# Block-sorted attention with a squared-ReLU layer: the last outputs in parts of 256, 128 and 128 columns, and the sorted values written to DRAM in two halves

## The chip, the cores and the metric

The kernel runs on one core of one Trainium2 chip. The metric is the device time of one execution in microseconds (us). The engines are named as the profile names them: PE (matrix engine), PEld (its weight loads), DVE (vector), ACT (scalar), POOL (GpSimd) and SP (sync). SP computes nothing here: it issues transfers and waits.

## What is computed

Inputs are q, k and v of shape 4 x 8 x 768 x 64 (batch, head, position, width) in float32, a sort_net of 4 x 8 x 8 x 8, and the weights of a layer from 512 to 2048 and back to 512. Each head's 768 positions are 8 blocks of 96.

```python
P = sort_net                                   # 5 rounds of exp, row and column normalization
for _ in range(5):
    P = np.exp(P - np.max(P, axis=-1, keepdims=True))
    P = P / (np.sum(P, axis=-1, keepdims=True) + 1e-09)
    P = P / (np.sum(P, axis=-2, keepdims=True) + 1e-09)
k_sorted = np.einsum('bhij,bhjcd->bhicd', P, k_b)      # blocks mixed by P
v_sorted = np.einsum('bhij,bhjcd->bhicd', P, v_b)
attn = softmax(q_b @ k_sorted^T / sqrt(64))            # within each block of 96
x = (attn @ v_sorted), heads side by side              # 3072 x 512
h = x @ w_in
g = s * np.maximum(h, 0)**2 + b
out = g @ w_out                                        # 3072 x 512
```

## The kernel before

The order of all instructions is written out by hand; every engine and SP's queue run theirs in the order of the program. The 3072 tokens are eight tiles t of 384 tokens (TG = 384): two for each of the four batches b, each of four blocks.

For a batch, k and v are mixed by P on PE (PD[b] holds P spread over 128 partitions). For batches 2 and 3 the sorted values go this way: `v_rows(b, u)`, six times, multiplies the v tile by PD on PE and DVE copies the product back over v (lines 349 and 351). Then `v_back(b)` writes that tile, RAW["v", b], to a DRAM tile vd in one transfer of 128 partitions x 6144 bytes (line 355), and loads it back in four transfers, one for each pair of z and e, into VS[b % 2] with positions on partitions (line 359). In vd the outermost index is e, then z. Each of the four loads moves 1536 rows of 128 bytes. Directly behind v_back on SP's queue stands `q_dma(b)`, two DMA transposes that make q ready for the scores (line 457), and behind these come the stores of the outputs. POOL's loads of the v of the batch after are held by a copy at line 90 until the transposed q is there.

The scores are `s_piece` (line 381: sc from qt and ks), the values `p_piece` (line 423: pv from vs and at), and two more transposes for each batch (line 449) make their result the input of the layer.

The layer is `ffn1(t)` (line 474, then ACT's relu and DVE's square into gt) and `ffn2(t)`. `ffn2` walks over three groups m of 128 tokens; each group is 16 matmuls of 512 columns into one PSUM tile ops (line 498), then `store`: DVE makes s * ops + bias into a tile ot of SBUF (line 519) and SP stores it (line 522). The pieces of the next batch's attention are put between the matmuls by a table of slots, of which batch 2 and 3 have theirs in tiles 2 to 5. The last two tiles, 6 and 7, have none. In the last tile (`last`) the third group, m = 2, is done as two groups of 16 matmuls of 256 columns (line 511), each with its own `store`.

Buffers that matter: ops comes from psb, two buffers; ot from osb, three, taken in turn, one for each call of `store`. vd has one, v's RAW tiles two.

How SP's transfers are watched: in the trace the landing of SP's transfers is told on eight semaphores, numbers 108, 109, 112, 113, 114, 116, 117 and 118, which they take in this order, in turn. A transfer is issued behind a wait for the one eight back, which used the same semaphore. At the program's end, SP waits for all eight, in the same order, and then for the other engines (line 673). Before, SP issues 52 transfers: sort_net, four of v, 25 output stores, two times one store of vd and four loads of vs, six transposes of q and six of x.

Of the kernel before, what the change touches and what calls it, by code (L numbers as in the profile page):

```python
# [9 lines left out]
FP = mybir.dt.float32  # L10
# [12 lines left out]
def kernel(  # L23
# [12 lines left out]
    nc = tc.nc  # L36
# [6 lines left out]
    d_model = H * D  # L43
    d_ff = moe_w_in.shape[1]
    NF = d_ff // 128
    HB = NB // 2
    TG = HB * BLK
# [22 lines left out]
    psb = ctx.enter_context(tc.tile_pool(name="psb", bufs=2, space=bass.MemoryType.PSUM))  # L70
# [9 lines left out]
    for c in range(0, C2, CV):  # L80
        nc.sync.dma_start(out=v0f[:, c:c + CV, :].rearrange("p c d -> p (c d)"),
                          in_=raw[2][0][:, c * D:(c + CV) * D])

    RAW = {}
# [123 lines left out]
    def q_banks(b, half, engs):  # L208
# [3 lines left out]
        for u in range(2):  # L212
# [13 lines left out]
            out=jsel, in_=ident.rearrange("p (h j z) -> p j h z", h=H, j=NB), axis=AX.XY, op=ALU.add),  # L226
        lambda: nc.vector.tensor_reduce(
            out=bm.rearrange("p (e z a) -> p e z a", e=2, z=2),
            in_=idv.rearrange("p a e j z -> p e z a j"), axis=AX.X, op=ALU.add),
# [122 lines left out]

    def v_back(b):
        vd = drp.tile([2, 2, NG, C2, D], BF, tag="vd", name="vd")
        nc.sync.dma_start(out=vd.rearrange("e z g c d -> (e z g) (c d)"),
                          in_=RAW["v", b].rearrange("p c d -> p (c d)"))
        for z in range(2):
            for e in range(2):
                nc.sync.dma_start(
                    out=VS[b % 2][z * GAP:z * GAP + C2, e * NG:(e + 1) * NG, 0:D],  # L360
                    in_=vd[e, z].rearrange("g c d -> c g d"))
# [130 lines left out]
    def ffn2(t, slots):  # L492
        gt = GT.pop(t)
        last = t == 2 * B - 1
        for m in range(TG // 128 - int(last)):
            ops = psb.tile([128, d_model], FP, tag="b", name="ops")
            for f in range(NF):
                nc.tensor.matmul(out=ops, lhsT=gt[:, f, m * 128:(m + 1) * 128],  # L498
                                 rhs=wo[:, f, :], start=(f == 0), stop=(f == NF - 1))
                if f % 4 == 3:  # L500
                    if f == NF - 1:
                        store(t, m, ops)
                    for p in slots.get(m * 4 + f // 4, ()):
                        p()
        if last:
            m = TG // 128 - 1
            for n0 in range(0, d_model, d_model // 2):
                ns = slice(n0, n0 + d_model // 2)
                ops = psb.tile([128, d_model // 2], FP, tag="b", name="ops")
                for f in range(NF):  # L510
                    nc.tensor.matmul(out=ops, lhsT=gt[:, f, m * 128:(m + 1) * 128],  # L511
                                     rhs=wo[:, f, ns], start=(f == 0), stop=(f == NF - 1))
                store(t, m, ops, ns)
# [3 lines left out]
    def store(t, m, ops, ns=slice(0, d_model)):  # L517
        ot = osb.tile([128, d_model], FP, tag="ot", name="ot")
        nc.vector.scalar_tensor_tensor(out=ot[:, ns], in0=ops, scalar=s_bc, in1=BIAS[0][:, ns],  # L519
                                       op0=ALU.mult, op1=ALU.add)  # L520
        r0 = t * TG + m * 128
        nc.sync.dma_start(out=out[r0:r0 + 128, ns], in_=ot[:, ns])
# [69 lines left out]
    def VB(b): return lambda: v_back(b)  # L592
# [36 lines left out]
    load("v", 2, 6, QT[1][:, NB - 1, 0, 0:1])  # L629
    s0, s1 = halves(1)  # L630
    ffn2(0, s0)
    ffn2(1, s1)
    for b in range(1, B):
        n = b + 1
        s0, s1, u0, u1 = {}, {}, {}, {}
        if n < B:
            load("k", n, 6, XT[2 * b + 1][:, HB - 1, NHP - 1, 0:1])
            load_q_rows(n)
            s0, s1 = halves(n)
            u0 = {i: [VRW(n, i)] for i in range(6)}  # L640
            u0[5] += [VB(n), QD(n)]
            if n + 1 < B:
                u0[5] += [LV(n + 1)]
        ffn1(2 * b, u0)
        ffn1(2 * b + 1, u1)
        ffn2(2 * b, s0)
        ffn2(2 * b + 1, s1)
# [30 lines left out]
```

## Time and profile before

| | |
|---|---|
| median of 3 runs | 223.43 us (222.94 to 223.51) |
| the profiled execution | 223.59 us |
| its span, first to last instruction | 221.8 us |
| granted PE clock over the span | 1.000 |
| v_back of batch 2: store of vd issued, last load of vs landed | 90.8, 109.35 us |
| v_back of batch 3: the same | 139.3, 157.12 us |
| output stores of 256 KB from 201.9 us on, issue to landing | 2.0 us |
| output stores of 128 KB, issue to landing | 1.7 us |
| last output store issued, landed, end of span | 218.95, 220.66, 221.8 us |

Times inside the execution are counted from the span's start. "Landing" is the last count on the transfer's semaphore. A line of a view of the profile gives line of the program, engine, operation, output and inputs by the program's names, shapes and the number of instructions. In the timeline the first two columns are start and length of a run of equal instructions, and in brackets stands the engine's idle time ahead of it and what ended it. SPq is SP's queue: its entries are issues of transfers and waits. In the list of waits the columns are the total, how many, and the longest. A matmul's recorded length contains its way through the array, so that those of a run overlap; the pitch, the distance between starts, is what one costs. The page puts PE at 97% of the span and the granted clock at full speed in each of its 40 slices.

### The profile page before, as it was taken

The page shows a single profiled execution, that of the slowest core. Times are in us where ns is not written, and L with a number is a line of the kernel's source. Part 1 is how long each engine was busy: PE and PEld are TensorE (multiplying, and loading weights), DVE is VectorE, ACT ScalarE, POOL GpSimd, SP SyncE. Part 2 cuts the span into 40 slices and gives each one's busy share as a digit, 9 for nine tenths or more (in the row PEclk, how much of TensorE's full clock was granted, in tenths as well). Part 3 has the DMA queues.
Part 4 walks back from the last instruction along what each step waited for, and adds up shares of the span by engine and source line. Part 5 has one row for each costly group of instructions (what it writes and reads, how often), then busy time and mean ns, then how long its engine had stood idle before and what let it go on. Part 6 is the DMA issues. An engine that isn't in the chain of part 4 may idle for free.

```text
span 221.8 us, 5257 instructions
## 1 busy us (share of the span) xinstructions
PE 214.8 (97%) x2212; PEld 129.6 (58%) x2231; DVE 123.3 (56%) x251; ACT 106.1 (48%) x144; POOL 70.6 (32%) x127
## 2 busy tenths in 40 slices
PE   7999999999999999999999999999999999999993
PEld 5977766555655555666446555655446556654453
DVE  6767457549754767546616677548417744442121
ACT  4677687656144344664622535665424355650000
POOL 7659791669914004930032008800000000000000
PEclk9999999999999999999999999999999999999999
DMA  6999999999999632999999546999911440001212
GB/s 154 280 165 126 125 162 207 204 177 117 116 182 165 183 96 46 138 236 127 91 252 171 138 121 91 236 147 92 221 69 50 121 120 0 0 3 47 95 47 95
DMA packets 66935, 28.92 MB, mean 130 GB/s; under 512 B 51808, under 2 KB 62816, under 8 KB 66912
## 3 DMA queue, kind: packets, MB, share of 16 engines
q0 software_dynamic: 31168, 12.85, 49.6%
q1 hardware_dynamic: 35744, 15.74, 34.3%
q8 instruction: 17, 0.28, 0.6%
q14 instruction: 6, 0.05, 0.1%
HBM read 28.85 MB, written 7.86 MB: 165 GB/s over the span
## 4 chain that ended last, share of the span: by engine, by line
PE 95%; DVE 2%; issue 1%; ACT 0%
PE hps L474 38%; PE ops L498 36%; PE z L132 5%; PE pv L423 4%; PE sc L381 3%; PE ops L511 2%; PE tv L330 2%; PE tp L294 1%; PE tpp L304 1%; PE tvr L349 1%; DVE vs L206 1%; PE tr L440 1%; PE scb L399 1%; PE sc L259 0%; PE pv L417 0%
## 5 line engine op out<-in xcount | busy, mean ns | idle before, releaser
L474 PE MATMUL hps<-xt,wi 128*128 128x384 bf16 x512 | 87.9, 326 | 0.0
L498 PE MATMUL ops<-wo,gt 128*128 128x512 bf16 x350 | 82.4, 379 | 1.5 <-issue 0.8
L486 ACT ACTIVATE rt<-hps 128x768 bf16<-128x768 f32 x64 | 51.8, 811 | 39.5 <-PE hps L474 38.8
L474 PEld LDWEIGHTS <-wi 128*128 128x128 bf16 x512 | 49.0, 98 | 32.6 <-issue 0.4
L487 DVE TENSOR_TENSOR gt<-rt 128x768 bf16<-128x768 bf16 x64 | 35.6, 558 | 41.2 <-ACT rt L486 41.0
L498 PEld LDWEIGHTS <-gt 128*128 128x128 bf16 x368 | 34.0, 98 | 37.2
L519 DVE SCALAR_TENSOR_TENSOR ot<-ops,s_bc,bias 128x512 f32<-128x512 f32 (+1 forms) x25 | 18.2, 729 | 37.9 <-PE ops L498 34.4
L389 ACT ACTIVATE at<-sc 112x768 bf16<-112x768 f32 x24 | 18.1, 808 | 31.8 <-PE sc L381 31.8
L429 DVE TENSOR_TENSOR x<-pv,rec 96x512 bf16<-96x512 f32 x32 | 22.0, 687 | 1.1
L116 POOL DMA_DIRECT2D qtok<-in_q_dram x24 | 18.6, 810 | 0.7 <-DMA rawk<-in_k_dram 0.6
L423 PEld LDWEIGHTS <-at 112*128 112x128 bf16 (+1 forms) x256 | 12.9, 101 | 6.7 <-ACT at L389 1.0
L142 POOL DMA_DIRECT2D wi<-in_moe_w_in_dram x24 | 13.0, 583 | 6.0 <-DMA qh<-in_q_dram 3.1
L423 PE MATMUL pv<-vs,at 112*128 112x66 bf16 (+1 forms) x256 | 13.9, 195 | 0.1
L93 POOL DMA_DIRECT2D rawk<-in_k_dram x21 | 11.2, 551 | 4.3 <-DMA rawv<-in_v_dram 2.0
L132 PE MATMUL z<-zeros 128*64 128x96 bf16 (+2 forms) x129 | 10.8, 257 | 1.3 <-DVE zeros L120 1.2
L93 POOL DMA_DIRECT2D rawv<-in_v_dram x18 | 9.7, 555 | 5.5 <-DMA wo<-in_moe_w_out_dram 4.7
L204 ACT CAST ks<-tpp 64x512 bf16<-64x512 f32 x12 | 8.7, 725 | 4.4 <-DVE ks L206 4.1
L132 PEld LDWEIGHTS <-zeros 128*64 128x64 bf16 (+1 forms) x130 | 8.5, 128 | 3.0 <-DVE zeros L120 1.2
L90 POOL COPY rawk<-xt 128x1 bf16<-128x1 bf16 x2 | 0.4, 190 | 31.1 <-DMA xt<-x 31.1
L428 DVE RECIPROCAL rec<-pv 96x8 f32<-96x8 f32 x32 | 6.4, 200 | 6.4 <-PE pv L423 6.4
L206 DVE CAST ks<-tpp 64x512 bf16<-64x512 f32 x12 | 8.7, 728 | 0.2
L351 DVE CAST rawv<-tvr 128x512 bf16<-128x512 f32 x12 | 8.2, 683 | 0.0
(93 smaller groups left out, 141.6 us busy)
## 6 DMA issues: line engine op xcount, KB each, us to landing
out_dram<-ot SPq DMA_DIRECT2D x23, 256.0 KB, 2.5
rawv<-in_v_dram POOLq DMA_DIRECT2D x18, 128.0 KB, 5.1
rawk<-in_k_dram POOLq DMA_DIRECT2D x18, 128.0 KB, 4.5
qtok<-in_q_dram POOLq DMA_DIRECT2D x24, 96.0 KB, 6.7
wo<-in_moe_w_out_dram POOLq DMA_DIRECT2D x4, 512.0 KB, 10.4
v0f<-in_v_dram SPq DMA_DIRECT2D x4, 384.0 KB, 7.1
vd<-rawv SPq DMA_DIRECT2D x2, 768.0 KB, 6.8
vs<-vd SPq DMA_DIRECT2D x8, 192.0 KB, 7.4
```

Of the source, the lines that this page charges most:

```text
L93: nc.gpsimd.dma_start(out=ti[:, c:c + n, :].rearrange("p c d -> p (c d)"), in_=raw["qkv".index(t)][b][:, c * D:(c + n) * D])
L116: nc.gpsimd.dma_start(out=ti[:, n + h], in_=qv[:, n + h])
L132: nc.tensor.matmul(out=z[0:m, 0:w], lhsT=zeros[:, 0:m], rhs=zeros[:, 0:w], start=True, stop=True)
L142: nc.gpsimd.dma_start(out=wi[:, al, f0:f1], in_=wiv[:, al, f0:f1])
L389: nc.scalar.activation(out=at, in_=sc[0:KR, :, 0:TG], func=AF.Exp, scale=scale)
L423: nc.tensor.matmul(out=pv[0:m, e, n * VW:(n + 1) * VW], lhsT=atf[:, c0:c0 + m], rhs=VS[b % 2][:, e * NG + g0 + n, :], start=True, stop=True)
L429: nc.vector.tensor_tensor(out=x[:, :, hp * 128:(hp + 1) * 128].rearrange("p n (e d) -> p e n d", e=2), in0=pvv[:, :, :, 0:D], in1=rec.unsq ...
L474: nc.tensor.matmul(out=H1[t, i][:, f, 0:TG], lhsT=wi[:, hp, fc:fc + 128], rhs=XT[t][:, :, hp, :], start=(hp == 0), stop=(hp == NHP - 1))
L486: nc.scalar.activation(out=rt, in_=h, func=AF.Relu)
L487: nc.vector.tensor_tensor(out=gt[:, 2 * i:2 * i + 2, :], in0=rt, in1=rt, op=ALU.mult)
L498: nc.tensor.matmul(out=ops, lhsT=gt[:, f, m * 128:(m + 1) * 128], rhs=wo[:, f, :], start=(f == 0), stop=(f == NF - 1))
L519: nc.vector.scalar_tensor_tensor(out=ot[:, ns], in0=ops, scalar=s_bc, in1=BIAS[0][:, ns], op0=ALU.mult, op1=ALU.add)
```

## The change

Three edits, in two functions.

In `v_back` the tile of sorted values is written to DRAM in two transfers of 64 partitions, one for each e, and the four loads go with e outermost, so that both loads of the first half come ahead of those of the second.

In `ffn2`, in the last tile, the output of the second group (m = 1) is evicted and stored in two halves of 256 columns; its matmuls stay 16 of 512 columns.

In the last tile's third group the two parts of 256 columns become three of 256, 128 and 128, each with its 16 matmuls, eviction and store.

```diff
     def v_back(b):
         vd = drp.tile([2, 2, NG, C2, D], BF, tag="vd", name="vd")
-        nc.sync.dma_start(out=vd.rearrange("e z g c d -> (e z g) (c d)"),
-                          in_=RAW["v", b].rearrange("p c d -> p (c d)"))
-        for z in range(2):
-            for e in range(2):
+        for e in range(2):
+            nc.sync.dma_start(out=vd[e].rearrange("z g c d -> (z g) (c d)"),
+                              in_=RAW["v", b][e * 64:(e + 1) * 64].rearrange("p c d -> p (c d)"))
+        for e in range(2):
+            for z in range(2):
                 nc.sync.dma_start(
                     out=VS[b % 2][z * GAP:z * GAP + C2, e * NG:(e + 1) * NG, 0:D],
                     in_=vd[e, z].rearrange("g c d -> c g d"))
...
                 if f % 4 == 3:
-                    if f == NF - 1:
+                    if f == NF - 1 and last and m == TG // 128 - 2:
+                        for n0 in range(0, d_model, d_model // 2):
+                            ns = slice(n0, n0 + d_model // 2)
+                            store(t, m, ops[:, ns], ns)
+                    elif f == NF - 1:
                         store(t, m, ops)
                     for p in slots.get(m * 4 + f // 4, ()):
                         p()
         if last:
             m = TG // 128 - 1
-            for n0 in range(0, d_model, d_model // 2):
-                ns = slice(n0, n0 + d_model // 2)
-                ops = psb.tile([128, d_model // 2], FP, tag="b", name="ops")
+            for n0, w in ((0, 256), (256, 128), (384, 128)):
+                ns = slice(n0, n0 + w)
+                ops = psb.tile([128, w], FP, tag="b", name="ops")
                 for f in range(NF):
                     nc.tensor.matmul(out=ops, lhsT=gt[:, f, m * 128:(m + 1) * 128],
                                      rhs=wo[:, f, ns], start=(f == 0), stop=(f == NF - 1))
```

SP then issues 56 transfers.

## The prediction

> **What bounds the kernel.** I read first the chain of work that ended last, by engine and line, and beside it the busy time of each engine.
>
> ```profile
> PE 214.8 (97%) x2212; PEld 129.6 (58%) x2231; DVE 123.3 (56%) x251; ACT 106.1 (48%) x144; POOL 70.6 (32%) x127
> PE 95%; DVE 2%; issue 1%; ACT 0%
> ```
>
> The chain is the matrix engine nearly from end to end. The list of PE's waits from 100 to 180 us, where both executions of v_back fall, has one entry, and it is not a wait for data:
>
> ```profile
> PE ops L498 <- issue: 0.3, 2, 0.2
> ```
>
> So nothing that v_back delivers makes PE wait now, and a faster v_back has nothing to give. What is left is the end of the span, where PE has run out. The timeline of the last stretch (start, length, engine, line, operation), then SP's waits from 215 us on (total, times, longest):
>
> ```profile
> 214.75 3.66 PE L511 MATMUL ops<-wo,gt 128*128 128x256 bf16 x32
> 214.95 0.75 DVE L519 SCALAR_TENSOR_TENSOR ot<-ops,s_bc,bias 128x512 f32<-128x512 f32 x1 [2.70 <-PE ops L498]
> 216.69 0.48 DVE L519 SCALAR_TENSOR_TENSOR ot<-ops,s_bc,bias 128x256 f32<-128x256 f32 x1 [1.00 <-PE ops L511]
> 218.44 0.48 DVE L519 SCALAR_TENSOR_TENSOR ot<-ops,s_bc,bias 128x256 f32<-128x256 f32 x1 [1.26 <-PE ops L511]
> ...
> 218.95 0.33 SPq L522 DMA_DIRECT2D out_dram<-ot  x1
> ...
> SPq L673 <- DMA out_dram<-ot: 1.1, 1, 1.1
> ```
>
> Behind PE's last matmul stands a serial tail: last eviction 218.44 to 218.92, last store issued 218.95, landed at 220.66 by its landing semaphore, span over at 221.8. The third part of it is SP's instructions at line 673, the program's end, from 220.6 to 221.0 us:
>
> ```profile
> L673 SPq EVENT_SEMAPHORE x5: 28/28/28, 220.7 to 220.9; - x5
> L673 SPq DRAIN  x1: 7/7/7, 221.0 to 221.0; - x1
> ```
>
> Before its last drain SP waits once for each of the eight landing semaphores, always in the order 108, 109, 112, 113, 114, 116, 117, 118. SP's 52 transfers take them in that order in turn, and the last is on 113, the fourth. So the wait that the landing ends is followed by four more, for transfers that landed long ago: 220.675 to 220.917, 0.242 us in which nothing is outstanding.
>
> **The change, part by part: the tail.** Times are from the one profiled execution.
>
> (a) PE. Two groups of 16 matmuls of 256 columns become one of 256 and two of 128. The 256-column pitch is (3.66 - 0.27) / 31 = 0.109 us. A matmul of 128 columns with a fresh 128x128 weight load is in the trace at line 304:
>
> ```profile
> 102.58 1.50 PE L304 MATMUL tpp<-pd,rawk 128*128 128x128 bf16 x24
> ```
>
> Its pitch is (1.50 - 0.22) / 23 = 0.056 us, so the added weight loads stay hidden. The second half began at 216.492; its 32nd narrow matmul starts at 216.492 + 31 x 0.0557 = 218.219, where the last wide one started at 218.130: +0.089. From that start to the eviction it was 0.311, of which the matmul's recorded length falls from 0.272 to 0.219: -0.053. The last eviction starts at 218.477, +0.036.
>
> (b) The last eviction. 512 columns took 0.751, 256 took 0.484, so 128 take 0.35: -0.134. The last store is issued at about 218.86 and not 218.95: **-0.098** with (a).
>
> (c) The last store's landing. The five stores of 256 KB from 201.9 us on took 2.01 us each, the two of 128 KB 1.72 and 1.71, so half as much again takes 1.57: **-0.145**. The packets agree: 2048 bytes took 86 ns, 1024 bytes 47, eight to each of the 16 engines. No 512-byte packet is in the tail, so the bounds are nothing (packets no cheaper than those of 1024 bytes) and -0.375 (the whole 8 x 47 ns gone); I take the line through both sizes, its nearest rows.
>
> (d) The wait ladder at line 673. SP issues 56 transfers and not 52: one more in each of the two v_backs, one more for the last tile's second store, one for its third. 56 is seven rounds of eight, so the last store is on 118, the last of the ladder; the seven waits before it pass while it is in flight. **-0.242**, or nothing if the semaphores are given out otherwise.
>
> Sum: -0.098 - 0.145 - 0.242 = **-0.485 us**; bounds -0.10 and -0.72.
>
> **New waits in the tail.** m = 1 of the last tile is evicted in two halves, 2 x 0.484 for 0.751, and stored from two buffers of ot. DVE is free for it: 214.95 to about 215.94, and its next work is at 216.69. But ot has three buffers. Before, the last two evictions reused buffers whose stores (208.82, 212.27) had long landed. Now the 128-column parts reuse those of m = 1's two halves. The first half's store is issued at about 215.46 and lands 1.72 later, 217.18; the part that needs it is ready at 216.492 + 15 x 0.0557 + 0.258 = 217.59: 0.41 us of cover. The second lands at about 217.69 and is needed at 218.48: 0.79. Behind a late landing stand on DVE only the last two evictions, on SP their stores. Without the cover, the last store goes back one for one.
>
> The eight-semaphore turn also makes each SP transfer wait for the one eight back. Counted through, those in the tail are stores from 178 us on and two transposes, all landed; in v_back and behind it they are transfers at least 5 us old. No cost.
>
> **v_back.** Each run issues two stores to DRAM of 64 rows for one of 128, then four loads, e outermost. One issue at line 355 takes 0.33 us, so +0.37 with its wait if the loads still wait for both halves; if a load waits for its own half alone, the first two go out before the second half has landed, earlier by up to the 7.4 and 6.1 us that the stores take. Behind it in SP's queue are the q transposes, then the stores of the first tile's outputs.
>
> ```profile
> L355 SPq DMA_DIRECT2D vd<-rawv x1: 327/327/327, 90.8 to 90.8; - x1
> ...
> 107.17 4.65 SPq L457 DMA_TRANSPOSE qt<-qtok  x2
> 111.91 6.83 SPq L522 DMA_DIRECT2D out_dram<-ot  x4
> ...
> 114.38 0.51 PE L381 MATMUL sc<-qt,ks 64*128 64x96 bf16 x16
> 117.43 0.43 PE L423 MATMUL pv<-vs,at 112*128 112x66 bf16 x8
> ```
>
> The last vs landed at 109.35, first read at 117.43: 8.1 us of cover. The two transposes landed at 112.22 and 113.83, first read at 114.38: 2.2 us on the one that holds the needed blocks, 0.55 if the reader waits for both. The second time it is 158.53 and 160.47 against 162.91. A delay of 0.37 fits under the smallest; an advance meets a PE that waits for nothing. Earlier transposes also let POOL's loads of the next v go earlier (POOL waited 17.1 us for them), away from nothing that PE needs. I take **0**.
>
> A rule speaks against this part: "DMA: Bandwidth & Descriptors" of the Trainium skill, Rules for kernel authors, says of two transfers to disjoint partition halves not to bother, since both spread over the same engines and run one behind the other, and to use one of 128 partitions. The same page gives about 2 us as the fixed cost of a transfer; if that came on top, an estimate by that page would have the second half 2 us late, and as the transposes stand last it would be cover that pays 2.2 or fails to pay 0.55. The trace of before has no such pair, so no row decides it.
>
> **The rivals.**
>
> R1, only the eviction gains: the 64 KB landing is no faster, or the ladder does not follow the turn, so that one or both of (c) and (d) fall away. For it: no 512-byte packet is shown. Against: the line through two sizes, and 52 transfers that keep the turn without an exception. At its end 223.43 - 0.10 = 223.33.
>
> R2, the slower side: each half store takes as long as the whole did, because rows from 64 partitions move at half the pace. Then in the first v_back the second half lands 7.4 us after the first, the last two loads and with them the transposes come some 6 us late, and PE stands at the first sc for about 6 - 2.2 = 3.8 us; in the second, 6.1 us and a cover of 4.4 (158.53 to 162.91) leave about nothing. 223.43 + 3.8 - 0.49 = about 226.7. It decides from a delay of 2.2 us on (0.55 if both transposes are waited for). For it: the DMA engines are shown 9 tenths busy around 90 us, so the stores are late already; against it: that load is POOL's qtok and k, and 7.4 us for 768 KB is a pace set by sharing, which halves would share too.
>
> R3, the packets vanish from the landing: (c) is -0.375 and the sum -0.72, 222.71.
>
> **How the numbers follow.** The profiled execution took 223.59 (span 221.8 and 1.8 around it); less 0.485 it is 223.10. It lies 0.16 above the median of the three runs, so against that the time is 223.43 - 0.485 = **222.95**. The forecast has 0.64, R1 0.14, R3 0.13, R2 0.09. A difference of 0.3% is 0.67 us, about what a measurement can tell from none; the gain is 0.22%, under it. The three runs of before lie 0.57 apart, so two medians can differ by some 0.3 without cause: a third of the forecast's share and most of R3's fall beyond 0.67. Faster 0.34, same 0.57, slower 0.09. Range 222.45 to 223.5: from R3 less that spread to R1 plus half of it; R2 is left out.
>
> **What would show it.** Right: the last SP store on the eighth semaphore with no wait behind its landing at line 673; landing to the end of the span 0.87 and not 1.11 us; last eviction near 0.35 us, last landing near 1.57, issued near 218.86; no PE wait from 100 to 180 us. Wrong: an eviction of the last two parts that waits for a store's landing; a narrow pitch over 0.06 us; a PE gap at line 381 near 114 or 163 us, which would be R2; more than 0.2 us gained before 214.7 us, which would be a gain in v_back that I deny.

## The result, and the profile after

The changed kernel took 222.82 us (median of 22 runs, 222.41 to 223.93), the kernel before beside it 223.41 (22 runs, 222.94 to 225.46): ratio 0.9973, interval 0.9962 to 0.9984, so 0.36 to 0.85 us less. Measured once more in the last experiment the ratio was 0.9986 (0.9974 to 0.9998). The forecast was 222.95 and a gain of 0.485.

The spans of the two profiled executions are 0.88 us apart, but most readings want them cut. The first cut is the first matmul of the layer (line 474 before, 475 after), the second the last matmul of 512 columns in the last tile, the third the first matmul of the last tile's second part. Between the second and the third lies the first part of 256 columns, 1.962 us both before and after. The stretch from the first cut to the second is called "the middle" from here on, and what lies behind the third "the end".

| us | before | after | difference |
|---|---|---|---|
| span's start to the layer's first matmul | 23.36 | 22.98 | -0.38 |
| from there to the last 512-column matmul of the last tile | 191.170 | 191.163 | -0.01 |
| the end: second part's first matmul to the span's end | 5.326 | 4.839 | -0.487 |

The third row is the change. The first is no work of it: the instructions there are the same, and it is taken up in the last section. The timeline of the changed kernel's last stretch (start, length, engine, line, operation, and in brackets idle time ahead and what ended it):

```profile
214.35 3.70 PE L516 MATMUL ops<-wo,gt 128*128 128x256 bf16 x48
214.56 0.88 DVE L524 SCALAR_TENSOR_TENSOR ot<-ops,s_bc,bias 128x256 f32<-128x256 f32 x2 [2.70 <-PE ops L499]
215.07 3.73 SPq L527 DMA_DIRECT2D out_dram<-ot  x5
216.30 0.48 DVE L524 SCALAR_TENSOR_TENSOR ot<-ops,s_bc,bias 128x256 f32<-128x256 f32 x1 [0.87 <-PE ops L516]
217.19 0.35 DVE L524 SCALAR_TENSOR_TENSOR ot<-ops,s_bc,bias 128x128 f32<-128x128 f32 x1 [0.41 <-PE ops L516]
218.09 0.35 DVE L524 SCALAR_TENSOR_TENSOR ot<-ops,s_bc,bias 128x128 f32<-128x128 f32 x1 [0.54 <-PE ops L516]
```

48 matmuls take 3.70 us where 32 took 3.66, and each of the last evictions waits for PE, none for a store. Then SP's instructions at the program's end, now line 678, from 218.8 to 219.4 us and from 219.9 on:

```profile
L678 SPq EVENT_SEMAPHORE  x8: 27/28/28, 218.8 to 219.3; - x8
...
L678 SPq EVENT_SEMAPHORE  x3: 17/17/28, 220.0 to 220.9; - x3
L678 SPq DRAIN  x3: 7/7/7, 220.1 to 220.4; - x3
```

Eight waits are through by 219.3 us, while the last store is in flight: one for other semaphores, and the first seven of the ladder. Of the three from 220.0 on, the first is the one that the landing (220.02) ends, and the first drain follows it at once. Before, five stood ahead of the first drain.

In the middle, PE's waits from 100 to 180 us:

```profile
PE ops L499 <- issue: 0.3, 2, 0.2
```

It is the line of before. The stores of vd, now line 356, in the first v_back and in the second:

```profile
L356 SPq DMA_DIRECT2D vd<-rawv x2: 525/552/578, 90.4 to 91.0; - x2
DMA to landing us min/median/max: 6.2/6.7/7.1
...
L356 SPq DMA_DIRECT2D vd<-rawv x2: 465/526/588, 138.9 to 139.4; - x2
DMA to landing us min/median/max: 6.8/7.2/7.6
```

A half of 384 KB takes 6.2 to 7.6 us to land, where the whole of 768 KB took 7.4 and 6.1.

### The profile page after: what moved, and what is told of

The parts are those of the page before. It is cut to its first block, busy times and chain, and to the rows that moved or that the text cites. A ratio compares the mean times of both kernels' runs of the same rounds, so it can differ in the third digit from the quotient of the medians.

```text
span 220.9 us, 5300 instructions
## 1 busy us (share of the span) xinstructions
PE 214.2 (97%) x2228; PEld 129.1 (58%) x2247; DVE 123.7 (56%) x253; ACT 106.0 (48%) x144; POOL 70.5 (32%) x127
## 4 chain that ended last, share of the span: by engine, by line
PE 90%; DMA 5%; DVE 1%; issue 1%; POOL 1%; ACT 0%; POOLq 0%
PE hps L475 38%; PE ops L499 36%; DMA rawk<-in_k_dram 5%; PE pv L424 4%; PE sc L382 3%; PE ops L516 2%; PE tv L330 2%; PE tpp L304 1%; PE tvr L349 1%; DVE vs L206 1%; PE tp L294 1%; PE tr L441 1%; PE scb L400 1%; POOL rawk L93 0%; PE sc L259 0%
## 5 line engine op out<-in xcount | busy, mean ns | idle before, releaser
L524 DVE SCALAR_TENSOR_TENSOR ot<-ops,s_bc,bias 128x512 f32<-128x512 f32 (+2 forms) x27 | 18.6, 691 | 38.0 <-PE ops L499 35.0
L132 PE MATMUL z<-zeros 128*64 128x96 bf16 (+2 forms) x129 | 9.9, 243 | 1.3 <-DVE zeros L120 1.2
L132 PEld LDWEIGHTS <-zeros 128*64 128x64 bf16 (+1 forms) x130 | 7.6, 117 | 3.1 <-DVE zeros L120 1.2
```

Of the source, the lines that this page charges most:

```text
L132: nc.tensor.matmul(out=z[0:m, 0:w], lhsT=zeros[:, 0:m], rhs=zeros[:, 0:w], start=True, stop=True)
```

## The experiments

All were read with the same cuts. In every execution profiled, but one, the middle was between 191.160 and 191.183 us; so the end is compared directly, and the times of whole runs are given with their ratio to the kernel before. Each end is read from one profiled execution. It repeats closely: the four executions with the changed kernel's tail and 56 transfers (the changed kernel twice, e5 and e9) gave 4.837 to 4.856.

**Each half of the change by itself.** In e1 v_back is as before; in e2 it alone is new.

```diff
 e1: the changed kernel
-        for e in range(2):
-            nc.sync.dma_start(out=vd[e].rearrange("z g c d -> (z g) (c d)"), ...
...
+        nc.sync.dma_start(out=vd.rearrange("e z g c d -> (e z g) (c d)"), ...
...
 e2: the kernel before
-        nc.sync.dma_start(out=vd.rearrange("e z g c d -> (e z g) (c d)"), ...
...
+        for e in range(2):
+            nc.sync.dma_start(out=vd[e].rearrange("z g c d -> (z g) (c d)"), ...
...
```

> The changed kernel with v_back as before: 54 transfers on SP, so the last store is on the sixth landing semaphore (116) and two waits follow its landing. The theory of the prediction (v_back gives nothing; eviction 0.098, landing 0.145, ladder 0.0605 for each wait taken from behind the landing) expects the end, from the first matmul of the last tile's second 256 columns to the span's end, to be 0.098 + 0.145 + 2 x 0.0605 = 0.36 us shorter than before (5.30 to 4.93), no change ahead of it beyond the execution's own spread, and about 223.05 us beside a before of 223.41. The rival that v_back gives part of the gain expects the stretch from 17 to 214 us longer than in the changed kernel by 0.1 us or more. The rival without the ladder expects 4.81, as in the changed kernel.

Measured: the end 4.968, middle 191.170, 223.10 us, ratio 0.9990 (0.9978 to 1.0001).

> The kernel before with the new v_back alone: 54 transfers, last store on the sixth semaphore. The theory expects from 17 to 214 us nothing (within 0.05 us), and at the end only the ladder, 2 x 0.0605 = 0.12 us, so about 223.3 beside 223.41. The rival that the halves help expects more than 0.2 us ahead of 214 us; the rival that they hurt (later landing of the second half) expects a gap of PE at the first scores of batch 2 or 3.

Measured: the end 5.209, middle 191.183, 223.48 us, ratio 1.0009 (0.9992 to 1.0025). In e1 the end is 0.358 shorter than before and in e2 0.117, as expected to the hundredth (the end of before is 5.326 and not 5.30, so the shortening is what can be compared), and the middle doesn't move: v_back gives the end two waits of the ladder by its two transfers and nothing else. The run times of e2 alone can't tell 0.12 us from nothing.

**The count alone.** e3 takes the changed kernel's last store one place further in the turn; e4 brings that of the kernel before to the last place. Both do it by storing one ot in two transfers: e3 for m = 0 of tile 6, e4 for four ots of tiles 6 and 7.

```diff
     def store(t, m, ops, ns=slice(0, d_model)):
...
-        nc.sync.dma_start(out=out[r0:r0 + 128, ns], in_=ot[:, ns])
+        k = 2 if (t, m) == (2 * B - 2, 0) else 1
+        w = (ns.stop - ns.start) // k
+        for c in range(ns.start, ns.stop, w):
+            nc.sync.dma_start(out=out[r0:r0 + 128, c:c + w], in_=ot[:, c:c + w])
```

> The changed kernel with one output store of tile 6 (m = 0) issued as two transfers of 256 columns: 57 transfers, so the last store is on the first semaphore and seven waits follow its landing. The ladder expects landing to span end 0.866 + 7 x 0.0605 = 1.29 us, 0.42 longer than in the changed kernel, nothing else changed; time about 0.42 above the changed kernel, near 223.25. The rival (the end gains by eviction and landing alone) expects the same as the changed kernel.

> The kernel before with four stores (tile 6, m = 0, 1, 2, and tile 7, m = 0) issued as two transfers each: 56 transfers, nothing else changed. The ladder alone expects landing to span end 0.866 and not 1.11 us: 0.242 gained, about 223.17 beside 223.41. The rival expects no difference.

Measured for e3: landing to the span's end 1.347 where the changed kernel has 0.918, the end 5.273, 223.44 us, ratio 1.0000 (0.9992 to 1.0009). One harmless transfer more, in the middle of a tile, makes the end 0.434 us longer than in the changed kernel. The 223.25 us expected were counted from the changed kernel's 222.82; beside 223.39 for the kernel before, measured with it, e3 gains nothing that a run time can show, and its end is 0.05 shorter than before. SP's instructions at its line 681 from 220.0 us on, with its last landing at 220.08:

```profile
L681 SPq EVENT_SEMAPHORE  x10: 17/28/28, 220.1 to 221.4; - x10
L681 SPq DRAIN  x3: 7/7/7, 220.6 to 220.9; - x3
```

The first drain comes 0.5 us behind the landing and not at once: seven more waits stand before it. For e4: landing to the end 0.918, the end 5.075, which is 0.251 less than before, 223.18 us, ratio 0.9988 (0.9979 to 0.9996). Its instructions there, at line 676, with a landing at 220.50, are those of the changed kernel again:

```profile
L676 SPq EVENT_SEMAPHORE  x3: 17/17/28, 220.5 to 221.4; - x3
L676 SPq DRAIN  x3: 7/7/7, 220.6 to 220.9; - x3
```

The rival without the ladder is out: two kernels that do the same work in the same order differ in the end by where the last transfer falls among eight. (The 1.29 and 0.866 of the expectations, and the 1.11 and 0.87 of the prediction, end at SP's last instruction, ahead of the span's end; to the last instruction of any engine before has 1.159, the changed kernel 0.918 and e3 1.347, so e3 lies 0.429 above the changed kernel where 0.42 was expected.)

**What the split of m = 1 is for, and what the narrow parts give.** Both edit the changed kernel and keep 56 transfers by e3's edit.

```diff
 e5:
-                    if f == NF - 1 and last and m == TG // 128 - 2:
...
-                    elif f == NF - 1:
+                    if f == NF - 1:
                         store(t, m, ops)
 e6:
-            for n0, w in ((0, 256), (256, 128), (384, 128)):
+            for n0, w in ((0, 256), (256, 256)):
```

> The changed kernel with m = 1 of the last tile evicted and stored whole again, and one store of tile 6 (m = 0) issued as two transfers so that there are 56 still. The theory (the split of m = 1 serves the count alone) expects the same end as the changed kernel: from the first matmul of the second part to the span's end 4.84 us, last landing 1.55, landing to end 0.92. The rival (the early half store takes load off the end) expects a later landing of the last store or an eviction that waits, 0.1 us or more.

> The changed kernel with its third group in two parts of 256 columns as before, and one store of tile 6 issued as two transfers, so that there are 56. The theory expects the ladder's gain kept (landing to end 0.92) and eviction and landing lost: 0.098 + 0.145 = 0.24 us longer than the changed kernel, 5.08 from the second part's first matmul to the span's end. If the two were not additive the end would differ from 5.08 by 0.05 us or more.

Measured for e5: the end 4.837, last landing 1.552, landing to end 0.917; 223.15 us, ratio 0.9982 (0.9968 to 0.9996). The split adds nothing but a transfer. For e6: the end 5.086, 0.247 longer than in the changed kernel, with 0.933 behind the landing; 223.40 us, ratio 0.9987 (0.9974 to 1.0000). So the narrow parts and the ladder add up. That is read from the end: by run time alone e6 can't be told from the changed kernel, whose second measurement has the ratio 0.9986.

**The cover of the three ot buffers.**

```diff
-    osb = ctx.enter_context(tc.tile_pool(name="osb", bufs=3))
+    osb = ctx.enter_context(tc.tile_pool(name="osb", bufs=2))
```

> The changed kernel with two buffers of ot and not three. The cover that the prediction named is then gone: by the changed kernel's times (second part's first matmul at 216.10) the 256-column eviction waits for the landing of m = 1's first half, 216.80 for 216.30, and the last eviction for the landing of the 256-column store, about 219.05 for 218.09. Expected: last store issued near 219.42, end 0.96 us later than in the changed kernel, 5.80 us from the second part's first matmul to the span's end; ahead of 214 us nothing beyond 0.1 us, since tile 2 to 5 have other work for PE. The rival (the buffers are not waited for, the landing is told earlier) expects 4.84.

Measured: the end 5.990, 224.25 us, ratio 1.0029 (1.0016 to 1.0042), so slower than before. The middle is 191.169. Its timeline at the end:

```profile
215.65 0.88 DVE L524 SCALAR_TENSOR_TENSOR ot<-ops,s_bc,bias 128x256 f32<-128x256 f32 x2 [2.70 <-PE ops L499]
218.00 0.82 DVE L524 SCALAR_TENSOR_TENSOR ot<-ops,s_bc,bias 128x256 f32<-128x256 f32 x2 [1.47 <-DMA out_dram<-ot]
218.54 1.05 PE L516 MATMUL ops<-wo,gt 128*128 128x128 bf16 x16 [0.28 <-DVE ot L524]
...
220.33 0.35 DVE L524 SCALAR_TENSOR_TENSOR ot<-ops,s_bc,bias 128x128 f32<-128x128 f32 x1 [1.51 <-DMA out_dram<-ot]
```

The line from 218.00 holds two evictions, the one of 256 columns and the first of 128. Two evictions now wait for a landing (`<-DMA out_dram<-ot`), as expected, and the price is 1.15 us and not 0.96. What was missed is the way from a landing to the eviction that it frees: 217.881 to 218.003 and 220.213 to 220.334, 0.12 us each time, where the expectation had 0.01 or 0.02; twice 0.1 is the 0.19 that lacks. PE waits as well, for the PSUM buffer that the held-up eviction reads: that eviction ends at 218.487, and the matmul behind it starts at 218.541. The third line gives 0.28 us for this; from start to start of the matmuls it is 0.504 where the pitch is 0.056, because the recorded length of the matmul ahead covers part of the wait. The last matmuls are done at 219.6, ahead of the 220.33 that the landing allows, so that wait costs nothing. The wait for the ring is real and three buffers cover it; with two, this change would have lost time.

**A narrower end still.**

```diff
-            for n0, w in ((0, 256), (256, 128), (384, 128)):
+            for n0, w in ((0, 256), (256, 128), (384, 64), (448, 64)):
```

with m = 1 whole and four buffers of ot.

> A version: m = 1 whole, third group in parts of 256, 128, 64 and 64 columns, four buffers of ot; 56 transfers. With a pitch near 0.030 us for 64 columns (eight matmuls of 66 columns at line 423 take 0.43 us in the timeline) the last matmul starts 0.09 later than in the changed kernel, the eviction is 0.067 shorter and starts 0.03 sooner behind its matmul, the landing 0.07 shorter if packets of 256 bytes go on along the line: 0.08 us gained, 4.76 from the second part's first matmul to the span's end. If weight loads set a pitch of 0.056 it is 0.7 us lost; if a packet of 256 bytes costs as much as one of 512, nothing is gained.

Measured: the end 4.840, no gain; 223.16 us, ratio 0.9990 (0.9970 to 1.0009). The expectation missed: of its terms the landing gave more (1.444, 0.109 less, not 0.07) and the eviction what was expected (0.284, 0.067 less), but the last matmul starts 0.20 later and not 0.09. Where that comes from stands in the timeline of the 32 matmuls of 64 columns and of the eviction of the part of 128:

```profile
216.90 0.63 PE L512 MATMUL ops<-wo,gt 128*128 128x64 bf16 x16
217.10 0.35 DVE L520 SCALAR_TENSOR_TENSOR ot<-ops,s_bc,bias 128x128 f32<-128x128 f32 x1 [0.41 <-PE ops L512]
217.50 0.63 PE L512 MATMUL ops<-wo,gt 128*128 128x64 bf16 x16
```

The pitch is as expected: (0.63 - 0.19) / 15 = 0.029 us in both parts, about half of the 0.0557 for 128 columns, though each matmul loads weights anew. But between the last start of the first row (217.334) and the first of the third (217.504) lie 0.170 us, 0.141 more than the pitch. The last part takes the PSUM buffer of the part of 128, as psb has two, and DVE's eviction of that part ended at 217.451, 0.053 ahead of the matmul; in e7 it was 0.054. The list of PE's waits doesn't show it, since the recorded length of the matmul ahead, 0.193, covers the gap. So what the expectation left out is the ring of two PSUM buffers. An estimate from this trace: with a third buffer the last matmul would come up to 0.14 us sooner and the last store about 0.10, as SP is through with issuing the store before it only near 218.38 (it issued the last at 218.48); the end would be near 4.74, about what was expected. That was not tried, so these runs don't show which width is best. In the changed kernel the same ring has room: the eviction of the 256 columns ends at 216.788, and the part that takes its buffer begins at 216.994.

**The smallest version.** e9 is the kernel before with the three parts of 256, 128 and 128 columns and the three stores of tile 6 in two transfers each, so 56; v_back and m = 1 are untouched. e10 is the changed kernel again, on the same chip.

```diff
-            for n0 in range(0, d_model, d_model // 2):
+            for n0, w in ((0, 256), (256, 128), (384, 128)):
...
-        nc.sync.dma_start(out=out[r0:r0 + 128, ns], in_=ot[:, ns])
+        k = 2 if t == 2 * B - 2 else 1
+        w = (ns.stop - ns.start) // k
+        for c in range(ns.start, ns.stop, w):
+            nc.sync.dma_start(out=out[r0:r0 + 128, c:c + w], in_=ot[:, c:c + w])
```

> The kernel before with nothing but the three parts of 256, 128 and 128 columns and the count: the three stores of tile 6 go as two transfers each, so that SP issues 56. v_back and m = 1 are as before. The theory (all of the gain is the narrower end and the place of the last transfer in the turn) expects the whole gain of the changed kernel: 4.84 us from the second part's first matmul to the span's end, the stretch from the first matmul of line 474 to the last of the 512-column ones at 191.16 to 191.18 us, and the same time as the changed kernel within what a measurement can tell. The rival (v_back or the split of m = 1 carries some of it) expects it 0.1 us or more slower in one of these two stretches.

> The changed kernel once more, on the chip of the kernel beside it: 4.84 us at the end and 191.16 between; what differs from its first profile is then the stretch ahead of the first matmul of line 474, which is expected anywhere from 22.9 to 24.1 us, as in the executions so far, whatever the kernel.

Measured for e9: the end 4.842, middle 191.163; 222.89 us beside 223.58, ratio 0.9970 (0.9959 to 0.9981). For e10: the end 4.856, 223.14 us, ratio 0.9986 (0.9974 to 0.9998), first cut at 23.34. e9 has the whole gain without any of the change to v_back; that it is faster than e10 is not shown, since the intervals overlap. The one number against the expectation is e10's middle, 191.243: 0.08 us more, which arise in the layer's first 16 matmuls and nowhere after; why is open.

## Why the prediction was right

Point by point, with the end of the two profiled executions counted from the second part's first matmul:

| step of the prediction | predicted us | measured us |
|---|---|---|
| (a), (b) last store issued | -0.098 | 2.461 to 2.368: -0.093 |
| (c) its landing | -0.145 | 1.706 to 1.553: -0.153 |
| (d) landing to span's end | -0.242 | 1.159 to 0.918: -0.241 |
| sum | -0.485 | -0.487 |

(a) The narrow pitch, taken from line 304, was 0.0557 as predicted, and the last eviction took 0.351 for 0.35. (c) Packets of 512 bytes took 27 ns, which the line through 86 and 47 puts at 28. R3, packets that vanish, is out.

(d) is shown by e3 and e4, which move the last transfer in the turn and leave the rest of the end and the middle as they were, and R1 falls with them and with the landing.

The new waits in the tail: the first of the two 128-column parts found its ot buffer free 0.40 us ahead (landing at 216.79, eviction at 217.19), the last one 0.82; predicted 0.41 and 0.79. e7 shows that the wait exists, and that 0.12 us pass between a landing and the eviction, so that 0.28 of the 0.40 us were to spare. The prediction counted the ot buffers and the semaphores, but not the two PSUM buffers, which the narrower parts also turn over faster. Here they were free 0.21 us ahead, so the omission cost nothing; in e8 it did.

v_back: nothing, by the middle of e1 and e2 against before. R2 did not come about, though half of its premise did: a half store takes about as long to land as the whole. But the two run beside each other and not one behind the other. In the first v_back of the changed kernel they land 6.2 us and 7.7 us after the first was issued (the whole: 7.4), in the second 6.8 and 8.1 (6.1). Each load waits for its own half, so the first two go out at 96.69, 6.3 us after the first store was issued; before it was 7.5. The last transpose lands at 112.89, 1.1 us ahead of the scores at 113.99 that read it, where it was 0.55. All of that stays inside the cover. The rule of the Trainium skill that the prediction weighed ("DMA: Bandwidth & Descriptors", Rules for kernel authors: don't bother with two transfers to disjoint partition halves) agrees with the runs in what it advises, since e9 does without the halves and loses nothing. Its reason, that the two run one behind the other, is not what the landings show: they are 1.5 and 1.3 us apart, where each half took 6.2 to 7.6. The 2 us that an estimate by the page's fixed cost, fitted there for transfers of GpSimd, put on top are not seen as such: the second half landed 0.3 and 2.0 us later than the whole had, counted from the first issue.

One reading in the prediction was wrong, without weight for the sum: 109.35 us was given as the landing of the last vs of the first v_back. It is that of the third of four; the last landed at 110.97, so the cover ahead of the first use was 6.5 us and not 8.1. The table of the profile before has the same slip for batch 2; for batch 3 its 157.12 is the fourth load's. A smaller slip: the waits for the eight semaphores stand ahead of the first of SP's three drains at the program's end, not of the last.

The total: 223.41 less 222.82 is 0.59, and the end accounts for 0.49. The rest is inside the interval, and every cut behind the first 23 us is accounted for, so nothing asks for a further cause. That the median came within 0.13 us of the forecast is in part luck: the second measurement of the same kernel has a ratio that puts the gain at 0.31 us (0.04 to 0.58), and the first 23 us alone vary by more than the gain. In the same way the sum of the end agrees to 0.002 because misses of 0.005 and 0.008 have opposite signs. What the experiments carry is the terms, each to about 0.01.

## What to carry to other kernels

A kernel that is bound by its matrix engine still ends in a serial tail: the last matmul group, its eviction, its store, and whatever the program waits for afterwards. Price that tail instruction by instruction, down to the waits behind the last landing; the place of the last transfer among the landing semaphores was worth as much as the narrower eviction and store together (0.24 us each), and one transfer more in a harmless place can give it all away. When an output is cut finer, count the buffers of its ring in SBUF against the landing times of the stores ahead of it, and those in PSUM against the evictions; and count from start to start of the matmuls, since a short wait can hide in their recorded lengths.

## What the runs showed of the hardware

The first 23 us differ between executions by more than the change is worth, whatever the kernel: the layer's first matmul came between 22.88 and 24.07 us in the twelve profiled executions, 22.98 and 23.34 in two of the same kernel. One part of that is PE's pace while it warms up on zeros. Its work on that tile from 4 to 6 and from 6 to 8 us, before, and then the same two stretches of the changed kernel (length, busy time and matmuls, granted clock, DMA share, GB/s):

```profile
4.00:6.00 2.00, 2.00 (x20) 1.00 1.16 285
6.00:8.00 2.00, 2.00 (x37) 1.00 1.15 311
```

```profile
4.00:6.00 2.00, 2.00 (x27) 1.00 1.14 283
6.00:8.00 2.00, 2.00 (x52) 1.00 1.15 315
```

PE is busy throughout, and the granted clock reads 1.00, yet by their starts the same 96-column matmuls go at a pitch of 80 ns at first and of 42.5 later. (The first matmuls on this tile have 256 columns; their pitch is 213 ns ahead of the step and 110 behind it.) The step came at 7.20 us before and at 5.36 after, and between 3.92 and 7.20 in all twelve, while PE started at about 1.2 us each time. "TensorE: Matmul & The Clock Gate" of the Trainium skill, in its part on the clock gate, tells of half the clock until PE has been busy for a window of about 3.4 us, with a transition that varies by 0.5 us either way; the halving agrees, but the steps lie 2.7 to 6.0 us behind PE's start, a spread of 3.3 us, which is wider than that. It doesn't decide alone: e5 had an early step, at 4.13 us, and its layer started at 23.51. PE's waits there from 11 to 24 us:

```profile
PE pe L259 <- DVE sn L245: 0.8, 1, 0.8
PE tkb L320 <- DMA rawk<-in_k_dram: 0.5, 1, 0.5
```

There the early pace ended in a wait of 0.8 us for DVE, and PE waited 0.5 us for the first loads of k; in the execution of before it waited for neither. How much of the spread each of the two carries was not tried.

With little else moving at the end, the landing of a store went by size from 2.01 us (256 KB) over 1.70 (128 KB) and 1.55 (64 KB) to 1.44 (32 KB in packets of 256 bytes, 17.6 ns each): eight times the bytes add 0.57 us, so most of the time does not grow with them.
